# A layer norm in a transformer block, worked on rows or on a feature-major copy of x

## The chip, the cores and the metric

The kernel runs on one core of a Trainium2 chip. TensorE (PE) multiplies matrices, VectorE (DVE), ScalarE (ACT) and GpSimd (POOL) work element by element, and SyncE (SP) issues the DMAs. Each engine takes its instructions in the order in which the program wrote them; semaphores tie the engines together. The metric is the device time of one execution in microseconds, and less is better.

## The reference

One transformer block in float32 for 2048 tokens with 448 features. The modulation (shift sa, scale ca, gate ga, and the same three for the second half) comes from a small vector c:

```python
sa, ca, ga, sb, cb, gb = (silu(c) @ w_mod) split in six
h = layernorm(x) * (1 + ca) + sa
x = x + ga * attention(h)         # 16 heads of 28, each token sees itself and 255 before it
h = layernorm(x) * (1 + cb) + sb
x = x + gb * (mish(h @ w1 + b1) @ w2)     # 448 -> 1792 -> 448
```

`layernorm` subtracts a token's mean over its features and divides by the root of its variance plus 1e-5. The change concerns the first `h` alone.

## The kernel before

Tokens are taken in four groups of 512, each of four tiles of 128. Float32 products are made of a high and a low part of each operand, and a 448-deep product of a tile then takes 11 matmuls (`passes`); so every `h` is kept as a high part `hh` and a low part `hl`, with features in partitions: four chunks of 128 features (the last 64 of them twice) by 512 tokens.

The first layer norm of a group goes like this. The rows of x (`xin`, 128 tokens x 448 features, four tiles) are loaded; DVE makes mean and variance of each tile (`ln_stats`), POOL the inverse root (L234, L235, a power); DVE normalises the rows in place (L241), POOL copies the last 64 features behind them (L224). Then PE transposes them, four 128x128 blocks into one PSUM bank `tr` for each chunk of features (`tr_chunk`, L250); ACT applies scale and shift and rounds to the high part (`hT_hi`, L257), DVE applies scale and shift to the bank (`hT_y`, L254) and subtracts the high part (`hT_lo`, L262). Group 0 does the same in its own code at the start, while weights arrive.

From `hh` and `hl` come the tiles of q, k and v of the group. Seven tiles `qk_0` to `qk_6` hold q and k with features in partitions; ACT and DVE split them into `st`, which is stored to DRAM (`scr`) and loaded again head by head (`q`, `k`). Four tiles `qk_v` hold v, and ACT and DVE evict them into `v` (DVE's part is L369). The tiles alternate between two PSUM banks of the tag `mm`, so a tile can begin only when the one two before it has been evicted.

A head then takes: scores `sA` for the row maxima (L679) and the maxima `mx` on DVE (L681); their transposes `mt`, cast to `mr` on DVE (L689, L690) and written into the operand q by a small DMA (`q<-mr`); scores again with the maximum and the mask inside (`sB`); the exponentials `P` and `Ph` on ACT, the low part `Pl` on POOL (L731); the product with v (`pv`). The 16 heads of a group are cut into 48 units of work, 192 in all. Between the units stand pieces of other work: the q, k and v tiles of the next group and the output projection of the group before (`fill_main`, handed out by a credit that grows by `RATE` with each unit), and small loads and element-wise work (`fill_side`). The order of instructions on every engine is the order of the program. All DMAs but one go through SP's queue (`dma`, L59); those of the fillers are put into the list `later` and issued at given places. After the heads, the MLP runs to the end (from 430 us on).

At the start the order is: the first q and k tiles of group 0, their stores, the loads of the first heads; then v0, v1, `qk_1`, v2, v3, `qk_5`, `qk_2`, with the scores `sA` of the first heads in between.

## Time and profile before

| | us |
|---|---|
| median of 3 runs | 710.71 (709.77 to 712.46) |
| profiled execution | 710.72 |
| its span in the trace | 708.9 |
| PE, DVE, ACT, POOL busy | 686.6, 385.2, 391.1, 327.0 |
| PE's 48 transposes of x in groups 1 to 3, busy | 7.3 |
| `hT_hi` on ACT, 16 in all, busy | 12.4 |
| `hT_y` (14) and `hT_lo` (16) on DVE, busy | 11.4 and 11.1 |
| normalisation of rows on DVE (12), busy | 11.2 |

The page shows one execution. A line of a group gives busy time, mean ns of one, and the engine's idle time before it with what ended it. The timeline gives start, duration and instruction, and in brackets how long the engine had been idle and what released it. Neighbouring instructions of one kind are drawn together (x4).

### The profile page before, as it was taken

How to read it: one execution, taken by the hardware profiler on the slowest of the kernel's cores; microseconds unless marked ns; L12 is line 12 of the kernel's file. 1: busy time of each engine (PE TensorE's matmuls, PEld its weight loads, DVE VectorE, ACT ScalarE, POOL GpSimd, SP SyncE). 2: the span in 40 equal slices, each digit the busy share in tenths (PEclk: the TensorE clock that was granted, in tenths of full speed). 3: DMA queues.
4: the chain of work that ended last, by engine and by line, in shares of the span. 5: the costliest groups of instructions: out<-in, count | busy, mean ns of one | idle time of the engine just before them, and what ended most of it. 6: DMA issues, size and time to landing. Idle time of an engine off the chain costs nothing.

```text
span 708.9 us, 12034 instructions
## 1 busy us (share of the span) xinstructions
PE 686.6 (97%) x4001; PEld 589.5 (83%) x4001; DVE 385.2 (54%) x1031; ACT 391.1 (55%) x740; POOL 327.0 (46%) x358
## 2 busy tenths in 40 slices
PE   9899999999999999999999799999999999999996
PEld 8677788888898788898887688888888888888885
DVE  5588667688664888555768744351324332532112
ACT  3628778767766858767877874343223322422221
POOL 6626779586766777666778947222010000000002
PEclk9999999999999999999999999999999999999999
DMA  7865764454662462763774155810250035001001
GB/s 211 253 226 181 226 198 150 137 161 150 192 216 66 153 207 76 195 200 92 226 216 128 54 192 166 228 29 1 104 119 1 0 104 119 1 12 41 1 1 52
DMA packets 75178, 90.16 MB, mean 127 GB/s; under 512 B 31535, under 2 KB 51741, under 8 KB 75117
## 3 DMA queue, kind: packets, MB, share of 16 engines
q1 hardware_dynamic: 74652, 89.39, 41.6%
q8 instruction: 32, 0.52, 0.3%
q14 instruction: 30, 0.24, 0.1%
q10 hardware_dynamic: 464, 0.00, 0.0%
HBM read 56.60 MB, written 32.51 MB: 126 GB/s over the span
## 4 chain that ended last, share of the span: by engine, by line
PE 71%; issue 11%; DVE 8%; ACT 2%; DMA 1%; POOL 1%; POOLq 0%; DVEq 0%; ACTq 0%
PE z L912 16%; PE pv L741 9%; PE qk L315 8%; PE sA L679 5%; PE acc L1097 5%; PE acc L1095 5%; PE acc L1096 5%; PE sB L709 5%; PE wo L315 4%; PE qk_v L315 4%; PE sB L720 3%; DVE junk L681 3%; PE et L755 2%; DVE tr L254 1%; ACT P L723 1%
## 5 line engine op out<-in xcount | busy, mean ns | idle before, releaser
L731 POOL TENSOR_TENSOR Pl<-P,Ph 128x512 fp32r<-128x512 f32 (+2 forms) x192 | 234.3, 1227 | 84.3 <-ACT Ph L724 46.1
L681 DVE CUSTOM_DVE_ANT_0 junk<-sA,mask 128x384 f32<-128x384 f32 (+2 forms) x256 | 135.3, 528 | 96.8 <-PE sA L679 88.1
L723 ACT ACTIVATE P<-sB 128x512 f32<-128x512 f32 (+2 forms) x192 | 109.7, 572 | 64.1 <-PE sB L720 59.0
L920 DVE TENSOR_TENSOR al<-t,ah 128x512 fp32r<-128x512 f32 x56 | 38.7, 692 | 178.8 <-ACT ah L919 178.8
L918 ACT ACTIVATE t<-z,b1c 128x512 f32<-128x512 f32 x56 | 38.4, 686 | 165.2 <-PE z L912 161.5
L724 ACT ACTIVATE Ph<-sB 128x512 fp32r<-128x512 f32 (+2 forms) x192 | 109.4, 570 | 0.0
L679 PE MATMUL sA<-k,q 84*128 84x384 f32 (+2 forms) x256 | 100.9, 396 | 2.8 <-DVE mx L681 1.5
L912 PE MATMUL z<-hlf,w 128*128 128x512 f32 x224 | 88.5, 395 | 0.0
L912 PE MATMUL z<-hhf,w 128*128 128x512 f32 x224 | 88.5, 395 | 0.0
L1095 PE MATMUL acc<-w2h,ah 128*128 128x448 f32 x224 | 82.0, 366 | 0.0
L1097 PE MATMUL acc<-w2h,al 128*128 128x448 f32 x224 | 81.9, 366 | 0.0
L1096 PE MATMUL acc<-w2l,ah 128*128 128x448 f32 x224 | 81.5, 364 | 0.0
L741 PE MATMUL pv<-Ph,v 128*60 128x256 f32 (+2 forms) x352 | 76.5, 291 | 3.6 <-DVE o L749 2.3
L741 PE MATMUL pv<-Pl,v 128*60 128x256 f32 (+2 forms) x352 | 73.6, 283 | 2.3 <-POOL Pl L731 2.3
L709 PE MATMUL sB<-q,k 86*128 86x256 f32 (+1 forms) x352 | 74.0, 284 | 0.2 <-DMA q<-mr 0.2
L912 PE MATMUL z<-hhf,w1l 128*128 128x512 f32 x168 | 66.2, 394 | 0.0
L709 PEld LDWEIGHTS sB<-q,k 86*128 86x128 f32 x352 | 61.5, 189 | 1.8 <-issue 0.8
L741 PEld LDWEIGHTS pv<-Ph,v 128*60 128x60 f32 x352 | 45.3, 133 | 18.2 <-ACT o L747 3.2
L720 PE MATMUL sB<-fdmask,identr 128*128 128x128 bf16 (+1 forms) x320 | 60.0, 253 | 0.0
L679 PEld LDWEIGHTS sA<-k,q 84*128 84x128 f32 x256 | 48.9, 192 | 9.1 <-DVE mx L681 6.0
L1106 POOL TENSOR_TENSOR yo<-yo,x 128x448 f32<-128x448 f32 x3 | 3.5, 1211 | 114.9 <-DVE yo L1104 114.9
L741 PEld LDWEIGHTS pv<-Pl,v 128*60 128x60 f32 x352 | 45.0, 131 | 10.8 <-POOL Pl L731 3.9
(161 smaller groups left out, 1291.6 us busy)
## 6 DMA issues: line engine op xcount, KB each, us to landing
scr<-st SPq DMA_DIRECT2D x24, 512.0 KB
k<-scr SPq DMA_DIRECT2D x48, 252.0 KB
q<-scr SPq DMA_DIRECT2D x64, 168.0 KB
scr<-st SPq DMA_DIRECT2D x32, 256.0 KB
x<-x1d SPq DMA_DIRECT2D x10, 448.0 KB
xin<-in_A_x_dram SPq DMA_DIRECT2D x8, 448.0 KB
xr<-in_A_x_dram SPq DMA_DIRECT2D x16, 224.0 KB
x1d<-xr SPq DMA_DIRECT2D x16, 224.0 KB
```

Of the source, the lines that this page charges most:

```text
L315: PE.matmul(p, b, a, start=(n == 0), stop=(n == 10))
L679: PE.matmul(p[:, c0:384], q[0:84, t * 128:(t + 1) * 128], k[0:84, t * 128 + c0:t * 128 + 384], start=True, stop=True)
L681: DVE.tensor_tensor_reduce(out=junk[:, c0:384], in0=p[:, c0:384], in1=mask[:, c0:384], scale=1.0, scalar=-3.0e38, op0=ALU.add, op1=ALU.max ...
L709: PE.matmul(p[:, c:c + 128 * (t1 - t0)], k[:, jj * 128:(jj + 1) * 128], q[:, t0 * 128:t1 * 128], start=(n == 0), stop=False, skip_group_ch ...
L723: ACT.activation(P[:, c0:], p[:, c0:], AF.Exp, scale=SCALE)
L724: ACT.activation(Ph[u][:, c0:], p[:, c0:], AF.Exp, scale=SCALE)
L731: eng.tensor_tensor(Pl[u][:, a:b], Pt[u][:, a:b], Ph[u][:, a:b].bitcast(F32), op=ALU.subtract)
L741: PE.matmul(pv[0:60, t0 * 128:t1 * 128], V[j % NV][:, h, :], P[u][:, c:c + 128 * (t1 - t0)], start=(P is Ph and b == 0 and n == 0), stop=F ...
L912: PE.matmul(zb[n], ps[m][1], ps[m][0], start=(m == 0), stop=(m == 10))
L1095: PE.matmul(p, ah[n][:, ts], w2h[f], start=(f == 0), stop=False)
L1096: PE.matmul(p, ah[n][:, ts], w2l[f], start=False, stop=False)
L1097: PE.matmul(p, al[n][:, ts], w2h[f], start=False, stop=(f == NF - 1))
```

## The change

The host passes a second copy `xt` of x, with features in partitions: for each group four chunks of 128 features (the last 64 twice) by 512 tokens. For groups 1 to 3 the rows are still loaded, but only for their statistics (`gen_rows`): four tiles `xr` of 128x448 in two buffers. Means and inverse roots (`mva`, 128x8) are stored to a small DRAM array `xms` and loaded back as two tiles `mb` in which every partition holds the value of all 512 tokens. Then (`gen_ln1`) POOL subtracts the mean from each chunk of `xt`, DVE multiplies by 1 + ca and by the inverse root, ACT adds sa and rounds to the high part `hx`, and DVE makes the low part `hy`. `hx` and `hy` have buffers of their own, one each, and the next group's are written when the last tiles that read them are in (`free`). The fillers wait for `ready`. Gone are the transposes, the rows' normalisation, POOL's copies, and the early load of group 1's `xin`; `RATE` of groups 1 and 2 is 0.83 and was 0.91. The statistics of group 1 are driven from the nine steps `fill0` at the start, those of group 2 and 3 from the units of the group two before. Line numbers shift: v's eviction on DVE is L369 before and L403 now, `Pl` L731 and L761.

```diff
-    x_load(0)
+    xin0 = qk.tile([128, 4, 512], F32, name="xin0", tag="hy")
+    for t in (0, 2):
+        dma(xin0[:, t:t + 2, 0:D], xf[t * 128:t * 128 + 256, :].rearrange("(t p) d -> p t d", p=128))
...
+    def gen_rows(g):
+        mv = qk.tile([128, 2, 4], F32, name=f"mva{g}", tag="mv", bufs=2)
+        rows = []
+
+        def load(t):
+            r = qk.tile([128, D], F32, name=f"xr{g}_{t}", tag="row", bufs=2)
+            later.append(lambda: dma(r, xf[g * GT + t * 128:g * GT + t * 128 + 128, :]))
+            rows.append(r)
+
+        load(0)
+        yield
+        load(1)
+        yield
+        for t in range(4):
+            flush()
+            ln_stats(rows[t], mv[:, :, t], qk, f"a{g}{t}")
+            if t < 2:
+                load(t + 2)
+            yield
+        POOL.tensor_scalar(mv[:, 1], mv[:, 1], EPS, None, op0=ALU.add)
+        POOL.tensor_tensor(mv[:, 1], mv[:, 1], mhalf, op=ALU.pow)
+        yield
+        later.append(lambda: dma(xms[g - 1].rearrange("a t p -> p (a t)"), mv))
+        yield
...
     def gen_ln1(g):
-        def xn_tiles():
-            return [xin[g][:, t] for t in range(4)]
-        for r in gen_ln([xin[g][:, t, 0:D] for t in range(4)], qk, xn_tiles, f"a{g}"):
-            if r:
-                XS[g] = r
+        drain(rows[g])
+        flush()
+        mb = [stg(qk, f"mb{g}_{a}") for a in range(2)]
+        ys = [stg(qk, f"xt{g}_{k}") for k in range(4)]
+        later.append(lambda: dma(ys[0], xt[g, 0]))
+        later.append(lambda: dma(mb[0], xms[g - 1, 0].rearrange("t p -> (t p)").partition_broadcast(128)))
+        yield
+        later.append(lambda: dma(ys[1], xt[g, 1]))
+        later.append(lambda: dma(mb[1], xms[g - 1, 1].rearrange("t p -> (t p)").partition_broadcast(128)))
+        yield
+        for k in (2, 3):
+            later.append(lambda k=k: dma(ys[k], xt[g, k]))
+        yield
+        yield
+        flush()
+        for k in range(5):
             yield "dve"
+            if k < 4:
+                POOL.tensor_tensor(ys[k], ys[k], mb[0], op=ALU.subtract)
+            if k:
+                DVE.scalar_tensor_tensor(ys[k - 1], ys[k - 1], cols[:, 1, k - 1:k], mb[1],
+                                         op0=ALU.mult, op1=ALU.mult)
+        while g not in free:
+            yield
+        hh, hl = HT[g] = new_H(g)
+        for k in range(5):
+            yield "dve"
+            if k < 4:
+                ACT.activation(hh[:, k], ys[k], AF.Identity, bias=cols[:, 0, k:k + 1])
+            if k:
+                DVE.scalar_tensor_tensor(hl[:, k - 1], ys[k - 1], cols[:, 0, k - 1:k],
+                                         hh[:, k - 1].bitcast(F32), op0=ALU.add, op1=ALU.subtract)
+        ready.add(g)
...
-    def gen_hT(g):
-        drain(ln1[g])
-        hh, hl = HT[g] = new_T(g, mid)
-        for ci in range(4):
-            p = bank("mm", 2, f"tr{g}{ci}")
-            tr_chunk(XS[g], ci, p)
-            pipe.add(2, lambda p=p, ci=ci: hT_hi(p, ci, hh, 0), lambda p=p, ci=ci: hT_lo(p, ci, hh, hl, 0))
-            yield 1.2
...
-    x_load(1)
     split_cols(*QCOLS[1], (DVE, DVE, None, None))
...
         if g + 1 < NG:
-            yield from gen_hT(g + 1)
+            while g + 1 not in ready:
+                yield
             yield from gen_qkv(g + 1, (0, 3, 4, 1) + VT)
...
-    RATE = {0: 0.56, 1: 0.91, 2: 0.91, 3: 0.65}
+    RATE = {0: 0.56, 1: 0.83, 2: 0.83, 3: 0.65}
...
     for _ in range(9):
         fill0()
+        next(rows[1], None)
...
+            if k == 2 and g < 2:
+                next(rows[g + 2], None)
```

The first place is DVE at the start of the attention, where v0 and v1 of group 0 are evicted (the first two rows with L369 before, L403 in the change). Before:

```order
L200 TENSOR_TENSOR wq_106<-wqs_111,wq_106 64x512
L369 TENSOR_TENSOR v_165<-qk_v_484,v_165 128x16x28
L369 TENSOR_TENSOR v_166<-qk_v_497,v_166 128x16x28
L681 ISA junk,mx_525<-sA_0_526,mask 128x128
L681 ISA mx_525 128x1
L220 BN_STATS sta_536<-xin_378 128x6
```

In the change, at the same place:

```order
L189 TENSOR_TENSOR wq_107<-wqs_112,wq_107 64x512
L209 BN_STATS sta_499<-xr_0_488 128x6
L210 BN_AGGR mva_487<-sta_499 128x2
L209 BN_STATS sta_510<-xr_1_494 128x6
L210 BN_AGGR mva_487<-sta_510 128x2
L403 TENSOR_TENSOR v_166<-qk_v_482,v_166 128x16x28
L209 BN_STATS sta_520<-xr_2_502 128x6
L210 BN_AGGR mva_487<-sta_520 128x2
L209 BN_STATS sta_526<-xr_3_513 128x6
L210 BN_AGGR mva_487<-sta_526 128x2
L403 TENSOR_TENSOR v_167<-qk_v_504,v_167 128x16x28
L711 ISA junk,mx_547<-sA_0_548,mask 128x128
```

The statistics of group 1's four row tiles stood between the row maxima of the first head and now stand ahead of both evictions.

The second place is SP's queue there. `q_1` and `k_3` are the operands of heads 2 and 3, `scr<-st_1` the store of the tile `qk_1`, and `q_0<-mr` the maxima of the first pair of heads. In the change:

```order
L59 DMA k_3_149<-scr 84x512
L59 DMA xr_0_488<-in_A_x_dram 128x448
L59 DMA xr_1_494<-in_A_x_dram 128x448
L59 DMA xr_2_502<-in_A_x_dram 128x448
L59 DMA xr_3_513<-in_A_x_dram 128x448
L59 DMA xms<-mva_487 128x8x1
L59 DMA xt_0_559<-in_xt_dram 128x512
L59 DMA mb_0_557<-xms 128x512
L59 DMA xt_1_560<-in_xt_dram 128x512
L59 DMA mb_1_558<-xms 128x512
L59 DMA scr<-st_1_545 128x2x512
```

Before, `scr<-st_1` follows k of head 3 at once, and the rows of group 1 (`xin_378`) are asked for ahead of the first store. The ten rows between are new here.

The third place is DVE between the scores of the second head and the cast of the maxima, in the change (`mb_1` is the inverse root in all partitions):

```order
L316 SCALAR_TENSOR_TENSOR xt_0_559<-xt_0_559,cols,mb_1_558 128x512
L711 ISA junk,mx_547<-sA_3_620,mask 128x384
L711 ISA mx_547 128x1
L403 TENSOR_TENSOR v_169<-qk_v_587,v_169 128x16x28
L316 SCALAR_TENSOR_TENSOR xt_1_560<-xt_1_560,cols,mb_1_558 128x512
L719 CAST mr_632<-mt_630 8x128
```

Before, the normalisations of rows (L241) stand at these places; now the products with `mb_1`, two of them ahead of the cast.

More of the change, by code (lines that the diff above doesn't have):

```diff
@@ L270, in adaln_block, with stg, new_H @@
     XS, HT = {}, {}
-    def gen_ln1(g):
-        def xn_tiles():
-            return [xin[g][:, t] for t in range(4)]
-        for r in gen_ln([xin[g][:, t, 0:D] for t in range(4)], qk, xn_tiles, f"a{g}"):
-            if r:
-                XS[g] = r
-            yield "dve"
+    def stg(pl, name):
+        return pl.tile([128, 512], F32, name=name, tag="stg", bufs=6)
+    free, ready = set(), set()
+    def new_H(g):
+        return (qk.tile([128, 4, GT], F32R, name=f"hx{g}", tag="hx"),
+                qk.tile([128, 4, GT], F32R, name=f"hy{g}", tag="hy"))
@@ L396, in adaln_block @@
     rs0 = st0.tile([128, 2, 4], F32, name="rs0")
-    xs0 = XS[0] = [xin[0][:, t] for t in range(4)]
+    xs0 = XS[0] = [xin0[:, t] for t in range(4)]
     for t in range(4):
@@ L527, in xr_tile @@
     def xr_tile(name):
-        return mid.tile([128, 512], F32, name=name, tag="xr", bufs=3)
-    def stg(pl, name):
-        return pl.tile([128, 512], F32, name=name, tag="stg", bufs=4)
+        return mid.tile([128, D], F32, name=name, tag="xr", bufs=3)
     def wm_load(i, k, pl, ws):
@@ L976, in side_step @@
             told[g] = next(side[g], None)
-    RATE = {0: 0.56, 1: 0.91, 2: 0.91, 3: 0.65}
+    RATE = {0: 0.56, 1: 0.83, 2: 0.83, 3: 0.65}
     FRONT = {0: 0, 1: 2, 2: 2, 3: 2}
+    rows = {g: gen_rows(g) for g in range(1, NG)}
     ln1 = {g: gen_ln1(g) for g in range(1, NG)}
@@ L992, in need @@
             pipe.step()
+            if g not in ready:
+                next(side[max(g - 1, 0)], None)
             try:
@@ L1192 @@
     arrays, args = {}, []
+    rows = [*range(D), *range(384, D)]
+    xt = _np.asarray(inputs["A_x"])[0].T[rows].reshape(4, 128, NG, GT).transpose(2, 0, 1, 3)
+    inputs = {**inputs, "xt": xt}
     for name in _INS:
```

28 lines of the change are left out of this document (7 added, 21 removed).

## The prediction

> **What bounds the kernel now.** I read the page's busy table first, then the stretches of the layer norms, then the opening in order of time.
>
> ```profile
> span 708.9 us, 12034 instructions
> PE 686.6 (97%) x4001; PEld 589.5 (83%) x4001; DVE 385.2 (54%) x1031; ACT 391.1 (55%) x740; POOL 327.0 (46%) x358
> ```
>
> TensorE is busy for 97% of the span, so nothing makes up later for time in which it stands still, and work taken off it counts if nothing else ends last there. The next view cuts the span; its columns after the stretch are its length and the busy time of PE, PEld, DVE, ACT and POOL.
>
> ```profile
> 29.50:65.00 35.50, 31.29 (x181) 24.48 (x180) 27.14 (x87) 17.70 (x38) 14.98 (x21) 1.00 0.61 209
> 169.00:180.00 11.00, 10.11 (x77) 8.64 (x76) 10.38 (x29) 10.05 (x20) 7.87 (x7) 1.00 0.35 101
> 271.00:282.00 11.00, 10.11 (x76) 8.57 (x75) 10.37 (x26) 10.01 (x19) 8.08 (x7) 1.00 0.32 100
> 430.00:709.00 279.00, 273.09 (x1263) 236.76 (x1261) 88.78 (x144) 86.80 (x136) 30.91 (x38) 1.00 0.21 58
> ```
>
> The two 11 us stretches hold the transposes of groups 2 and 3: DVE and ACT are as full there as PE. Those of group 1 end the first stretch, where PE idles 4.2 us. The last 279 us are the MLP, which the change leaves alone. In the opening, everything hangs on small things in order of time:
>
> ```profile
> 30.51 1.16 DVE L369 TENSOR_TENSOR v<-qk_v,v 128x448 fp32r<-128x448 f32 x2
> 31.19 0.50 PE L315 MATMUL qk<-hh,wq 128*128 128x512 f32 x1 [1.10 <-DVE v L369]
> 34.90 0.30 PE L679 MATMUL sA<-k,q 84*128 84x128 f32 x1 [0.91 <-DMA k<-scr]
> 35.03 0.42 PE L315 MATMUL qk_v<-wq,hh 128*128 128x448 f32 x1
> 47.98 0.33 PE L709 MATMUL sB<-q,k 86*128 86x384 f32 x1
> ```
>
> PE starts the tile after v0 and v1 (31.19) the moment that DVE has evicted v0 and a PSUM bank is free. The tile v2 (35.03) needs v1's bank. 47.98 is the first score tile with its row maximum, from which the exponentials and all later units run.
>
> **The change part by part.** *Transposes, the gain.* The groups of the lines view give busy time and mean ns:
>
> ```profile
> L250 PE MATMUL tr<-ident,xin 128*128 128x128 f32 x48 | 7.3, 274 | 1.6 <-DVE hl L262 1.6
> L241 DVE TENSOR_SCALAR xin<-xin,mva,rsa 128x448 f32<-128x448 f32 x12 | 11.2, 929 | 0.5 <-POOL rsa L235 0.5
> ```
>
> 48 times 274 ns would be 13 us, but starts count on a pipelined engine, not durations:
>
> ```profile
> 53.63 0.60 PE L250 MATMUL tr<-ident,xin 128*128 128x128 f32 x4
> 53.98 0.42 PE L679 MATMUL sA<-k,q 84*128 84x384 f32 x1
> ```
>
> Four take 0.35 us to the next start and up to 0.44 on the chain of waits, so twelve groups of four give 4.2 to 5.3 us; I take 4.9. A third of that lies where PE idled anyway, so I take off 0.5. The 1.6 us that PE waited for DVE's `hl` goes too: two reads of a tile in PSUM (L254, L262) become reads of SBUF off PE's path. Gain 6.0 us, bounds 3 (the stretches stay bound by DVE and ACT, which get 24 new full-width operations on DVE for 36 old ones) and 8.
>
> *Row loads on DVE's queue, the main loss.* Before, group 1's rows (`xin`) were asked for at 20.83, and DVE's statistics stand behind both v evictions and the first row maximum. Now, by the order of instructions, the rows `xr` are issued on SP only after the loads of heads 2 and 3, and on DVE the statistics of xr_0 and xr_1 stand ahead of v0's eviction, those of xr_2 and xr_3 ahead of v1's.
>
> ```profile
> GB/s 211 253 226 181 226 198 150 137 161 150 192 216 66 153 207 76 195 200 92 226 216 128 54 192 166 228 29 1 104 119 1 0 104 119 1 12 41 1 1 52
> ...
> 20.83 1.03 SPq L59 DMA_DIRECT2D xin<-in_A_x_dram  x2
> 31.70 0.32 SPq L59 DMA_DIRECT2D k<-scr  x1
> 41.14 0.39 SPq L59 DMA_DIRECT2D k<-scr  x1
> 35.55 0.62 DVE L220 BATCH_NORM_STATS2 sta<-xin 128x6 f32<-128x448 f32 x1
> 36.21 0.18 DVE L221 BATCH_NORM_AGGREGATE mva<-sta 128x2 f32<-128x6 f32 x1
> ```
>
> The last of those head loads was issued at 41.14 to 41.53, having waited for stores to land. 896 KB of `xin` no longer runs ahead of the stores, worth 0 to 3.6 us at 253 GB/s (the second of the page's 40 slices); I take 1.5. So xr_0 is issued at 40.0 and xr_1 at 40.4. A load lands 3.2 us after its issue (31.70 to PE's start at 34.90), so 43.6 for a slightly larger one, and 44.2. With 0.62 + 0.18 for each, DVE reaches v0's eviction at 45.0 and ends it at 45.6 (0.58 each): PE starts at 45.6 what it started at 31.19, 14.4 us late. The `row` tag has two buffers, so xr_2 can be asked for only when xr_0 has been read (44.2), and xr_3 at 45.0; they land at 47.8 and 48.6, statistics end at 49.4, v1's eviction at 50.0. v2 starts at 50.0, not 35.03: 15.0 us late.
>
> *The bounce through DRAM, on top.* Now `mva` goes through POOL's power, to DRAM as 1024 single numbers of 4 bytes, and back as two broadcasts; no row here has that store. Nearest is the load of c, 448 numbers of 4 bytes, issued at 0.72 and used at 5.03, that is 4.3 us.
>
> ```profile
> 40.64 0.23 POOL L234 TENSOR_SCALAR rsa<-mva 128x4 f32<-128x4 f32 x1 [8.89 <-DVE mva L221]
> 40.96 1.04 POOL L235 TENSOR_TENSOR rsa<-rsa,mhalf 128x4 f32<-128x4 f32 x1
> 0.72 0.46 ACTq L83 DMA_DIRECT2D cT<-in_c_dram  x1
> 5.03 0.20 ACT L168 ACTIVATE sT<-cT 112x4 f32<-112x4 f32 x1 [2.54 <-DMA cT<-in_c_dram]
> 44.80 0.27 DVE L689 CAST mr<-mt 8x128 fp32r<-8x128 f32 x1
> 45.09 1.48 SPq L59 DMA_DIRECT2D q<-mr  x2
> L731 POOL TENSOR_TENSOR Pl<-P,Ph 128x512 fp32r<-128x512 f32 x155 | 201.1, 1302 | 76.3 <-ACT Ph L724 40.6 <-PE pv L741 10.4 <-PE sA L679 7.9
> L920 DVE TENSOR_TENSOR al<-t,ah 128x512 fp32r<-128x512 f32 x56 | 38.7, 692 | 178.8 <-ACT ah L919 178.8
> ```
>
> Power done at 50.7; the store between 3.2 (any load) and 9.8 (4.3 scaled by 1024/448), taken as 5.0 since part of 4.3 is fixed: 55.9 with its issue. SP waits there for it, and all behind it wait: xt_1, the stores of st_1, then `q<-mr`. The means land 3.4 us later at 59.3. POOL subtracts xt_0 in 1.3 (a subtraction of this size, L731): 60.6. DVE then has, ahead of the cast of the row maximum, the product of xt_0 (0.69 as L920), a maximum (0.6), v3's eviction (0.6) and the product of xt_1 (0.69, its subtraction ready at 61.9): the cast starts at 63.4. From cast to score tile took 47.98 - 44.80 = 3.2, so 66.6 against 47.98: **18.6 us late**, in place of the 15.0 and not beside it. The bounds are 14.8 (relief 3.6, store 3.2) and 24 (no relief, store 9.8). PE's order up to there has the same number of rows as before, so nothing is caught up. For groups 2 and 3 the rows are read tens of units ahead and the bounce is hidden behind PE's fillers; if that cover failed, each would cost a store and a broadcast, some 8 us.
>
> The Trainium skill ("TensorE: Matmul & The Clock Gate", Part 1) says that an idle window of about 3.4 us puts TensorE at half its clock, and that the return takes about as long. By that page such a stall would end with a slow stretch, for which I estimate, from its figures, 1.7 us of lost work. No run here has idle time of that length after the start, so it is not in the sum.
>
> *POOL, the second loss.* Twelve subtractions at 1.30 replace twelve copies of 0.3. In groups 1 and 2 they stand between the `Pl` of units in which POOL is already back to back:
>
> ```profile
> L224 POOL COPY xin<-xin 128x64 f32<-128x64 f32 x16 | 5.0, 315 | 5.5 <-DVE xin L241 3.4 <-ACT xin L407 0.9 <-PE qk L315 0.7
> ...
> 142.33 3.90 POOL L731 TENSOR_TENSOR Pl<-P,Ph 128x512 fp32r<-128x512 f32 x3
> 143.67 0.45 PE L741 MATMUL pv<-Pl,v 128*60 128x256 f32 x2 [0.40 <-POOL Pl L731]
> ```
>
> PE already waits 0.40 for POOL there. Four times 1.3 less 4 x 0.3 is 4 us a group; POOL's idle time nearby takes most. I take 2.5 for both, bounds 0 and 6. ACT's four `hx` per group (from SBUF, not PSUM) replace four `hh` of the same size: nothing, with 10.05 of 11 us in its stretch as the cover that then goes. The changed rate of fillers moves PE's work, and removes none: nothing.
>
> Sum against the profiled run's own 710.72 (span 708.9 and 1.8 around it; the runs' median is 710.71): 710.7 + 18.6 - 6.0 + 2.5 = 725.8, rounded to **725.5**.
>
> **Rivals.** *Short bounce.* The store takes no longer than a load and the relief is whole: 14.8 in place of 18.6, so 722. For it: 1024 numbers are little data. Against it: 4.3 us for 448 of them.
>
> *DVE and POOL hold each other up.* L241 takes 498 ns at its shortest and 1493 at its longest, always the same shape:
>
> ```profile
> L241 DVE TENSOR_SCALAR xin<-xin,mva,rsa x12: 498/852/1493, 42.0 to 256.6; 128x448 f32<-128x448 f32 x12
> ```
>
> If each of the 16 new DVE operations of groups 2 and 3, which read two SBUF tiles, puts 1.0 us on POOL or itself, and half of that lies on the path: +8, so 733.5. Against it: these stretches lose the L241 that show it. The Trainium skill ("SBUF — State Buffer", section on the two separate sides) calls the port pair of the two engines an exclusive lock, the loser waiting out the whole instruction, also for DVE operations with two SBUF inputs. L241's longest of 1493 agrees with a wait of about one operation.
>
> *The other side: the rows come in time.* If xr_0 to xr_3 landed by 29, statistics would be done before v0 and v1 need evicting and the mean's broadcast by 41: no stall, and 710.7 - 6.0 + 2.5 = 707 (704 to 709). It decides where the loads are issued: from about 25 us on, each later us is a us lost, since DVE's statistics stand ahead of the evictions. For it: the removed `xin` leaves that place free. Against it: SP's rows start in the order of the program (31.70, 41.14, 45.09), and there the loads stand behind k of head 3.
>
> **How the numbers follow.** Forecast 0.73 (its own range 721 to 730), short bounce 0.09, mutual blocking 0.13, rows in time 0.05. The range 715 to 736 goes from the smallest stall with the largest gain (710.7 + 14.8 - 8 = 717, and a little for overlap of refilling) to the largest stall with a gain of 3 and a POOL loss of 4 (735.7). A measurement here can tell 0.5%, that is 3.6 us, from no change. Faster: the last rival, 0.04. Within: its upper end and the lowest stalls, 0.03. Slower: 0.93.
>
> **What would show it.** In the profile after: PE idle for some 14 us from 31, released by DVE's v eviction, and DVE's idle time there released by the load of `xr`; `sB` first at 64 to 68; the groups' `tr` gone from 53 to 63, 169 to 176 and 271 to 278; POOL's subtractions of about 1.3 among the `Pl`; everything from about 70 us on late by a constant less the gains. It is wrong if PE runs through 31 to 45, if the first `sB` is at 50, or if the stretches between 120 and 280 lose more than 6 us.

## The result and the profile after

The changed kernel takes 757.11 us (median of 4 runs, 756.62 to 761.02) against 711.17 us for the kernel before beside it (709.77 to 712.46): 1.066 of its time, with an interval of 1.062 to 1.070. The forecast was 725.5, with 736 as the upper end of the range. So the direction was right and the loss three times what was forecast: 46 us and not 15. The profiled execution took 756.62 us, 45.9 more than the one of before.

The head of the page, to be set beside that of before:

```profile
span 754.8 us, 11984 instructions
...
PE 693.9 (92%) x3953; PEld 595.5 (79%) x3953; DVE 383.4 (51%) x1019; ACT 390.5 (52%) x740; POOL 343.0 (45%) x358
...
PEclk9966998998999998999999999999999999999999
```

TensorE has 48 matmuls fewer, the transposes, and yet 7.3 us more of busy time (693.9 for 686.6); its idle time went from 22.3 to 60.9 us. Idle time is 38.6 of the 45.9 us. The rest is busy time made longer: PEclk has two 6s over the opening (third and fourth slice, 38 to 75 us), where before the granted clock stood at 1.00 in the stretch from 29.5 to 65.

**The opening.** TensorE, then DVE, then SP's queue, in order of time:

```profile
46.87 0.80 PE L349 MATMUL qk<-hx,wq 128*128 128x512 f32 x1 [16.37 <-DVE v L403]
...
71.30 0.38 PE L717 MATMUL mt<-ident,mx 128*8 128x128 f32 x1 [11.90 <-DVE mx L711]
...
77.21 0.34 PE L739 MATMUL sB<-q,k 86*128 86x384 f32 x1
```

```profile
44.73 0.63 DVE L209 BATCH_NORM_STATS2 sta<-xr 128x6 f32<-128x448 f32 x1 [13.84 <-DMA xr<-in_A_x_dram]
...
46.22 0.59 DVE L403 TENSOR_TENSOR v<-qk_v,v 128x448 fp32r<-128x448 f32 x1
...
69.18 1.59 DVE L316 SCALAR_TENSOR_TENSOR xt<-xt,cols,mb 128x512 f32<-128x512 f32 x1 [11.21 <-DMA mb<-xms]
...
73.40 0.27 DVE L719 CAST mr<-mt 8x128 fp32r<-8x128 f32 x1
```

```profile
40.83 5.61 SPq L59 DMA_DIRECT2D xr<-in_A_x_dram  x4
...
51.10 0.38 SPq L59 DMA_DIRECT2D xms<-mva  x1
...
63.86 0.33 SPq L59 DMA_DIRECT2D mb<-xms  x1
```

There are two waits. TensorE idles 16.37 us up to 46.87 for v0's eviction on DVE, and DVE idles 13.84 us in front of its statistics for the rows `xr`, which SP issued at 40.83. Then the small store of means and inverse roots is issued at 51.10, and the load that reads it back at 63.86: 12.75 us apart. DVE idles 11.21 us in front of its first product for that load, the row maxima stand behind it on DVE, and TensorE idles 11.90 us for them. The first score tile with its maximum starts at 77.21, where it started at 47.98.

The chain of waits names the same two places:

```profile
40.83 3.87 DMA xr<-in_A_x_dram
...
51.10 12.75 DMA xms<-mva
```

**Where the 45 us come in.** I took the first score tile `sA` of each head in both traces; the table gives by how much it starts later than in the kernel before. z is the first tile of the MLP.

| start of | before, us | later after the change, us | gained since the row above |
|---|---|---|---|
| head 0 | 34.9 | 16.8 | 16.8 |
| head 3 | 48.3 | 29.2 | 12.4 |
| head 12 | 88.7 | 30.5 | 1.3 |
| head 15 | 103.3 | 37.3 | 6.8 |
| head 21 | 136.9 | 36.4 | -0.9 |
| head 23 | 148.6 | 42.3 | 5.9 |
| head 37 | 238.7 | 40.7 | -1.6 |
| head 39 | 250.3 | 46.0 | 5.3 |
| z | 411.2 | 45.2 | -0.8 |

The lag comes in five steps. The first two are the opening. The others belong to groups 2 and 3, whose work was forecast to be covered. Between the steps the lag also drifts: after head 23 it goes on to 45.6 at head 31 and is back at 40.7 at head 37, with no long wait in between. The fillers of these groups are handed out more slowly than before (`RATE`), so a difference of a few us inside a group is not by itself a cost. Here is the third step in a view of stretches (columns: stretch, length, busy time of PE, PEld, DVE, ACT, POOL, granted clock, DMA share, GB/s), and under it TensorE and SP:

```profile
116.00:120.00 4.00, 4.00 (x28) 3.31 (x28) 2.97 (x12) 3.71 (x10) 2.71 (x4) 1.00 0.38 17
120.00:124.00 4.00, 4.00 (x27) 3.21 (x26) 1.66 (x7) 2.45 (x7) 2.55 (x3) 1.00 0.65 26
124.00:129.00 5.00, 0.88 (x5) 0.36 (x3) 0.24 (x2) 0.64 (x2) 1.26 (x1) 0.78 0.79 232
129.00:133.00 4.00, 3.80 (x14) 3.20 (x15) 0.58 (x3) 2.15 (x6) 1.01 (x1) 0.50 0.90 323
```

```profile
129.20 0.66 PE L739 MATMUL sB<-q,k 86*128 86x384 f32 x1 [4.32 <-DMA q<-mr]
...
182.83 0.66 PE L709 MATMUL sA<-k,q 84*128 84x384 f32 x1 [3.78 <-DMA k<-scr]
...
288.11 0.66 PE L709 MATMUL sA<-k,q 84*128 84x384 f32 x1 [2.91 <-DMA k<-scr]
```

```profile
112.86 0.39 SPq L59 DMA_DIRECT2D xms<-mva  x1
...
120.09 5.33 SPq L59 DMA_DIRECT2D q<-mr  x2
```

Group 2's store is issued at 112.86. From 116 to 124 the DMA engines are counted as busy for 0.38 and 0.65 of the time and move 17 to 26 GB/s; then they move 232 and 323. The `q<-mr` issued at 120.09 lands too late, and TensorE idles 4.32 us. After that it works at half clock: 14 matmuls in 4 us, where there were 28 before the wait. Heads 22 and 38 wait in the same way for `k<-scr`, 3.78 and 2.91 us.

The single packets of this trace tell more. The 1024 pieces of 4 bytes are noted with some 9 ns each, and nearly all of them start between 114 and 116 us. What is slow comes after them: a 2 KB packet of another transfer takes 92 ns on average from 112.9 to 116, 790 ns from 116 to 124, and 102 ns from 124 to 129. So the pieces do not fill the engines by their own time; for 8 us after them everything else crawls. Where they are held in these 8 us the trace does not show.

Group 3's store (issued at 217.09) has the same form, and the engines again move only 7 GB/s from 224 to 228. But little else is asked for there, and TensorE waits 0.44 us:

```profile
229.78 0.47 PE L739 MATMUL sB<-q,k 86*128 86x384 f32 x2 [0.44 <-DMA q<-mr]
```

That gave four suspects to take apart: the place of the row loads, the store of 4-byte pieces, the queue in which k's small store and load stand, and the clock.

### The profile page after: what moved, and what is told of

It reads as the page before. It is cut to its first block, busy times and chain, and to the rows that moved or that the text cites. A ratio compares the mean times of both kernels' runs of the same rounds, so it can differ in the third digit from the quotient of the medians.

```text
span 754.8 us, 11984 instructions
## 1 busy us (share of the span) xinstructions
PE 693.9 (92%) x3953; PEld 595.5 (79%) x3953; DVE 383.4 (51%) x1019; ACT 390.5 (52%) x740; POOL 343.0 (45%) x358
## 4 chain that ended last, share of the span: by engine, by line
PE 66%; issue 11%; DMA 11%; DVE 6%; POOL 2%; ACT 2%; SPq 1%; POOLq 0%; ACTq 0%; DVEq 0%
PE z L942 15%; PE pv L771 8%; PE qk L349 5%; PE sA L709 4%; PE acc L1135 4%; PE acc L1133 4%; PE acc L1134 4%; PE sB L739 4%; PE wo L349 4%; PE qk_v L349 4%; DMA xms<-mva 3%; PE sB L750 3%; DMA scr<-st 2%; DMA q<-mr 2%; DVE junk L711 2%
## 5 line engine op out<-in xcount | busy, mean ns | idle before, releaser
L761 POOL TENSOR_TENSOR Pl<-P,Ph 128x512 fp32r<-128x512 f32 (+2 forms) x192 | 236.8, 1240 | 95.5 <-ACT Ph L754 63.8
L771 PE MATMUL pv<-Ph,v 128*60 128x256 f32 (+2 forms) x352 | 78.4, 297 | 3.7 <-DVE o L779 2.3
L739 PE MATMUL sB<-q,k 86*128 86x256 f32 (+1 forms) x352 | 76.0, 290 | 6.2 <-DMA q<-mr 6.2
L709 PEld LDWEIGHTS sA<-k,q 84*128 84x128 f32 x256 | 50.5, 199 | 16.0 <-issue 7.1
L349 PE MATMUL qk<-hx,wq 128*128 128x512 f32 x100 | 41.7, 417 | 16.4 <-DVE v L403 16.4
```

The lines of the kernel that those rows point to most:

```text
L349: PE.matmul(p, b, a, start=(n == 0), stop=(n == 10))
L709: PE.matmul(p[:, c0:384], q[0:84, t * 128:(t + 1) * 128], k[0:84, t * 128 + c0:t * 128 + 384], start=True, stop=True)
L739: PE.matmul(p[:, c:c + 128 * (t1 - t0)], k[:, jj * 128:(jj + 1) * 128], q[:, t0 * 128:t1 * 128], start=(n == 0), stop=False, skip_group_ch ...
L761: eng.tensor_tensor(Pl[u][:, a:b], Pt[u][:, a:b], Ph[u][:, a:b].bitcast(F32), op=ALU.subtract)
L771: PE.matmul(pv[0:60, t0 * 128:t1 * 128], V[j % NV][:, h, :], P[u][:, c:c + 128 * (t1 - t0)], start=(P is Ph and b == 0 and n == 0), stop=F ...
```

## The experiments

### The store by itself, and each opening wait by itself

First the store was put alone into the kernel before: a tile of zeros, 128 partitions by 8, written to DRAM at unit 24, with nothing that reads it. Once it goes out in the layout of the change, 1024 pieces of 4 bytes; once as 128 pieces of 32 bytes.

```diff
+    pbd = dram.tile([2, 4, 128], F32, name="pbd")     # second probe: [128, 8]
+    pb = qk.tile([128, 8], F32, name="pb", tag="pb")
+    POOL.memset(pb, 0.0)
...
+        if u == 24:
+            dma(pbd.rearrange("a t p -> p (a t)"), pb)  # second probe: dma(pbd, pb)
```

> The kernel before, with one store added that nobody reads: 1024 numbers of 4 bytes from a 128x8 tile to DRAM, each to an address of its own, at the place where the changed kernel stores the means of group 2 (behind k of head 10's loads, ahead of the stores of qk_3). Theory A (the small pieces hold the DMA engines for some 10 us, whatever waits for the store): almost no other packets for about 9 us after it, the next maxima q<-mr land late, PE waits about 4 us there as in the changed kernel, and the time rises by 4 to 7 us, to about 716. Theory B (PE's loss there comes from the other loads and stores that the change added or moved): no gap, within 1 us of before.

> The same added store at the same place, the same 4 KB, but each partition's 8 numbers go to one piece of 32 bytes: 128 pieces, not 1024. Theory A with a cost for each piece: an eighth of the hold, about 1.3 us, and PE hidden from it: 711 to 712. If a store to DRAM of any form stops the queue there, as much as with 1024 pieces, 715 to 718.

The 4-byte store costs 720.52 us, 1.012 of before (1.006 to 1.018); the 32-byte store 712.26, 1.001 (0.999 to 1.002), which can't be told from no change. The same 4 KB in the same place cost some 8.5 us or nothing. SP's queue and TensorE with the 4-byte store; then SP's queue with the 32-byte store; then the kernel before:

```profile
83.52 0.82 SPq L59 DMA_DIRECT2D pbd<-pb  x1
...
93.13 3.17 SPq L59 DMA_DIRECT2D q<-mr  x2
```

```profile
98.17 0.64 PE L713 MATMUL sB<-q,k 86*128 86x384 f32 x1 [4.46 <-DMA q<-mr]
```

```profile
82.91 0.67 SPq L59 DMA_DIRECT2D pbd<-pb  x1
...
88.49 1.48 SPq L59 DMA_DIRECT2D q<-mr  x2
```

```profile
89.58 1.49 SPq L59 DMA_DIRECT2D q<-mr  x2
```

Nobody reads `pbd`, and yet TensorE idles 4.46 us for the next `q<-mr`. The stretch from 88 to 95 us with the 4-byte store and in the kernel before, columns as above:

```profile
88.00:95.00 7.00, 5.72 (x36) 4.04 (x34) 2.83 (x11) 4.42 (x10) 4.21 (x4) 1.00 0.94 112
```

```profile
88.00:95.00 7.00, 7.00 (x46) 5.22 (x44) 3.29 (x15) 5.28 (x13) 4.05 (x5) 1.00 0.69 206
```

The DMA engines are counted as busier than before (0.94 for 0.69) and move about half (112 GB/s for 206): the small pieces delay whatever shares the engines with them. The loss is above the 4 to 7 us that theory A expected. The step in the start of the heads is 7.1 us by head 15 and 8.1 at head 63. It is the third step of the table above (6.8), made in a kernel that has nothing else of the change.

Then each of the two opening waits was mended in the changed kernel. The first run loads group 1's four row tiles in the place in which the kernel before loaded `xin`, all at once, into buffers that are free there. The second has TensorE transpose the 128x8 means and roots, so that the store goes out as eight pieces of 512 bytes, in all three groups.

```diff
-            r = qk.tile([128, D], F32, name=f"xr{g}_{t}", tag="row", bufs=2)
+            r = stg(qk, f"xr{g}_{t}")[:, 0:D]           # group 1 only
...
+    rows = {g: gen_rows(g) for g in range(1, NG)}       # ahead of the first st stores
+    next(rows[1])
+    flush()
```

```diff
-        later.append(lambda: dma(xms[g - 1].rearrange("a t p -> p (a t)"), mv))
+        if g > 1:
+            yield
+        p = bank("tr", 1, f"mw{g}")
+        PE.transpose(p[0:8, 0:128], mv.rearrange("p a t -> p (a t)"), ident)
+        mw = qk.tile([8, 128], F32, name=f"mw{g}", tag="mw")
+        ACT.activation(mw, p[0:8, 0:128], AF.Copy)
+        yield
+        later.append(lambda: dma(xms[g - 1].rearrange("a t p -> (a t) p"), mw))
```

> The changed kernel, with one thing undone: the four row tiles of group 1 are asked for ahead of the first stores of q and k, where the kernel before asked for them (into four buffers that the means and xt use later). The order on DVE stays, statistics ahead of v0's eviction. Forecast's theory (DVE's queue is held by the late row loads): PE's wait of 16.4 us at 30.5 falls below 2; the store of the means goes out behind the loads of head 3 at about 41, and the first sB starts at about 66 to 68 instead of 77.2, so 746 (743 to 749). Rival (the wait at 30 is for something else in v's eviction, such as its ACT half): 755 to 758.

> The changed kernel with one thing changed: the means and inverse roots (128x8) are turned on PE and stored as 8 pieces of 512 bytes instead of 1024 of 4 bytes, in all three groups. The row loads stay late. Theory A: the first wait of PE stays at 16 us; from the store to the first load of the means 3 us instead of 12.7; first sB at about 68 instead of 77.2; the step of 5 to 7 us between heads 12 and 15 is gone; time about 741 (738 to 745). Theory B (a round trip through DRAM and the broadcasts cost this much in any form): 752 to 758.

With the rows early, 745.00 us, 1.046 (1.039 to 1.053); with the store in eight pieces, 737.79, 1.036 (1.028 to 1.044). Beside the 757.11 of the change they win 12 and 19 us, as the first theory of each run has it; the time with the large pieces is just below its range. TensorE with the rows early, then SP's queue and TensorE with the large pieces (line numbers have moved by a few in both):

```profile
33.60 0.50 PE L356 MATMUL qk<-hx,wq 128*128 128x512 f32 x1 [4.02 <-DVE v L410]
...
58.27 0.38 PE L727 MATMUL mt<-ident,mx 128*8 128x128 f32 x1 [12.77 <-DVE mx L721]
```

```profile
50.80 0.29 SPq L59 DMA_DIRECT2D xms<-mw  x1
...
52.02 0.33 SPq L59 DMA_DIRECT2D mb<-xms  x1
```

```profile
45.98 0.79 PE L356 MATMUL qk<-hx,wq 128*128 128x512 f32 x1 [16.10 <-DVE v L410]
...
60.12 0.27 PE L724 MATMUL mt<-ident,mx 128*8 128x128 f32 x1 [1.43 <-DVE mx L718]
```

Each mends its own wait and leaves the other: 16.37 us become 4.02 (below 2 was expected) with the second wait at 12.77; and 11.90 become 1.43 with the first at 16.10. From the store to the load that reads it are 1.2 us instead of 12.75. In starts of heads, the early rows bring head 0 to 2.6 us late in place of 16.8. The large pieces bring head 3 to 17.3 in place of 29.2, and their step from head 12 to head 15 is 0.4 us, not 6.8. The steps at heads 21 to 23 and 37 to 39 stay in both (store in large pieces: 7.1 and 4.5), so they have another cause.

### Both mendings, the queue, and the clock

> Both mendings in the changed kernel: group 1's rows asked for early, and the means stored in pieces of 512 bytes. If the row loads and the small store are two separate causes, their gains add: PE's first wait below 4 us, the second (12 us) gone too, first sB at 51 to 54, time 757 - 12 - 19 = about 724 (721 to 728). If one hides behind the other: 733 or more. The steps of 4 to 7 us at heads 22 and 38 stay.

Both together: 731.50 us, 1.028 (1.023 to 1.033). The waits that are left in the opening:

```profile
35.44 0.38 PE L302 MATMUL mw<-ident,mva 128*8 128x128 f32 x1 [5.03 <-POOL mva L297]
...
51.82 0.37 PE L734 MATMUL mt<-ident,mx 128*8 128x128 f32 x1 [3.31 <-DVE mx L728]
```

The first is of the experiment's own making: the transpose of the means stands in TensorE's order ahead of work that was ready, and waits there for POOL's power. Head 3 is 9.3 us late. If the gains of 12.1 and 19.3 simply added, the time would be 725.7; the result lies between the two expectations. A mending has a place in a queue too.

For the steps at heads 22 and 38, one edit on top of it: the store of a finished q and k tile goes to the front of the list of waiting DMAs, ahead of the loads of `xt`, of means and of rows.

```diff
-            later.append(put)
+            later.insert(0, put)
```

> The same, and in addition a finished q or k tile's store to DRAM goes to the head of the list of waiting DMAs, not to its end, so that it is issued ahead of xt, the means and the row loads that wait there. Theory C (heads 22 and 38 wait for k because its store stands in SP's queue behind some 1.2 MB of xt, means and rows, and k's load right behind the store): the steps of 7.1 and 4.5 us there shrink to below 2 each, time about 715 (712 to 719). Rival (the added bytes hold the DMA engines wherever the store stands, or PE waits there for POOL, whose subtractions of the mean stand between the Pl): 721 to 728.

It gives 728.72 us, 1.024 (1.020 to 1.028), far from the 715 of theory C. The step at heads 21 to 23 goes from 5.9 to 5.3, that at 37 to 39 from 5.2 to 1.7; in the opening the same edit costs, for head 3 is now 12.9 us late in place of 9.3. SP's load of k for head 22 and TensorE's wait for it:

```profile
152.25 0.35 SPq L59 DMA_DIRECT2D k<-scr  x1
...
159.59 0.66 PE L726 MATMUL sA<-k,q 84*128 84x384 f32 x1 [2.39 <-DMA k<-scr]
```

The order of issue accounts for most of the step at 38 and little of that at 22. The intervals of the two kernels overlap, so the 2.8 us between their medians are not shown by the times; the move of the step is in the traces. Why k still comes late at 22 can be read from SP's queue in this trace: the store goes out at 147.74, but k's load is issued at 152.25, behind five loads of `xt`, means and rows (148.69 to 151.31, 1.2 MB), and TensorE starts on k only at 159.59. So the store no longer stands behind these loads, and k's load still does. No run moved that load.

For the clock, transposes of the identity matrix into a spare bank were put into the two opening waits of the changed kernel, 140 and 105 of them. They compute nothing that is used, and keep TensorE working.

```diff
+    wb2 = bank("pv", 1, "warm2")
...
+            for _ in range(140):                        # ahead of qk_1
+                PE.transpose(wb2[:, 0:128], ident, ident)
...
+            for _ in range(105):                        # ahead of the first mt
+                PE.transpose(wb2[:, 0:128], ident, ident)
```

> The changed kernel, with 140 transposes of the identity (never read) put ahead of the tile qk_1, where PE stands still for 16.4 us, and 105 ahead of the first turning of the maxima, where it stands 11.9 us; at 0.11 us each they end about when the waits end. If the low granted clock after the waits (0.53 in 47 to 52 us, 0.75 in 71 to 80) comes from the idle time, the 11 matmuls behind the first wait start 0.23 us apart instead of 0.43, those behind the second as well, the clock reads 1.0 there, and 2 to 4 us are won: 753 to 755. If the clock has no part in the loss: 757.

756.87 us, 1.064 (1.059 to 1.068): the same as the change. The stretch behind the first wait, in the change and then with the transposes, and under them the stretch behind the second wait with the transposes:

```profile
47.00:52.00 5.00, 5.00 (x13) 3.96 (x14) 2.08 (x5) 0.10 (x1) 1.27 (x2) 0.53 0.23 75
```

```profile
47.00:52.00 5.00, 4.72 (x24) 3.92 (x23) 3.38 (x11) 0.60 (x1) 1.27 (x2) 1.00 0.20 50
...
71.00:75.00 4.00, 4.00 (x13) 3.24 (x13) 3.50 (x8) 0.60 (x1) 2.98 (x2) 0.57 0.07 19
```

Behind the first wait the granted clock is 0.53 in the change and 1.00 with the transposes; matmuls of that tile start 0.43 us apart and 0.23 apart, and 24 fit in the stretch that held 13. So the half clock is real; but TensorE only reaches the next wait sooner, whose end is set by the means. Behind the second wait the run did not do what was expected: the transposes ended early, TensorE still idled 1.96 us, and the clock fell to 0.57 (0.50 in the change). The MLP starts 44.2 us late in place of 45.2. So the half clock behind the first wait costs nothing in the times; what it costs behind the second, where no other wait follows at once, was not measured.

### Can the stall be ordered away?

Three kernels move the pieces of the last mending. In `mended`, group 1's statistics are driven between the row maxima of group 0's first heads, with the transpose of the means one step later, so that neither v's evictions on DVE nor TensorE stand behind them. In `mended2` the statistics come right behind v1's eviction, and the loads of the rows of groups 2 and 3 begin four heads later. `mended3` also holds back `xt` and the means of group 1 until the first `q<-mr` are issued.

```diff
+            if next(rows[1], 0) == 0:                   # mended: in the loop of the first scores
+                side_step(0)
...
+    for _ in range(5):                                  # mended2: behind the nine steps fill0
+        next(rows[1])
...
-            if k == 2 and g < 2:                        # mended2
+            if k == 2 and g < 2 and s % H >= 4:
...
-            if next(rows[1], 0) == 0:                   # mended3
+            if next(rows[1], 0) == 0 and i == 2:
```

> All three mendings (rows early, pieces of 512 bytes, stores first), and in addition the statistics of group 1 stand between the row maxima, behind v0's and v1's evictions, as in the kernel before. If late rows, small store and late k stores were all that cost, the start is as before (first sB at 48 to 49), and what is left is the forecast's gain from the transposes less POOL's share: 6.0 - 2.5, so 706 to 711, against 712 for the kernel before on this chip. If 24 new operations on DVE and 12 on POOL cost as much as the transposes: 711 to 714. If something else still stands in the way: above 715.

> The last kernel (723) with two things placed otherwise. Its own trace shows POOL's low parts waiting 3.0 us at head 4 behind a subtraction of the mean whose load was late, and q<-mr late at head 16 behind loads. Here the four statistics of group 1 stand right behind v1's eviction, where DVE was idle for 3.7 us before, so the means go out some 5 us earlier; and the row loads of groups 2 and 3 begin four heads later, away from xt and the means of the group ahead. If order alone is left as the cause: the step of 5.2 us at heads 4 and 5 and the 7.2 us at heads 16 to 18 are gone, the waits at heads 21 and 37 below 1 us, time 708 to 713 against 711 to 712 before. If the added operations and 3.6 MB of loads cost it wherever they stand: 716 to 722.

> The last kernel (724, whose PE stands 7.0 us at 53.3 for the first q<-mr) with one thing moved: the loads of xt and the means of group 1 (1.5 MB) are issued behind the first q<-mr, a store of the means and the loads of head 4, not ahead of them. Theory D (a small load that PE needs at once lands late when a megabyte has been issued before it): the 7.0 us wait and the half clock behind it (2 us) go, first sB at 48 to 49, and the lag at heads 3 and 4 falls from 7.7 to below 2; time 714 to 718. Rival (q<-mr is late because DVE's cast of the maxima is, or POOL's subtractions then hold the Pl for as long): 721 to 726.

All three take the same time: 723.41 us (1.018, 1.014 to 1.023), 723.97 (1.019, 1.015 to 1.022) and 723.41 (1.016, 1.013 to 1.020). For none of them does the time fall in the range in which order, or one late load, was all that was left; `mended2` is above its rival's range too. The place where it is lost moves. Lag of the heads, as above:

| start of head | 0 | 3 | 6 | 12 | 15 | 19 | 23 | 39 |
|---|---|---|---|---|---|---|---|---|
| mended | -0.4 | -0.8 | 5.0 | 3.7 | 4.0 | 11.3 | 13.6 | 12.9 |
| mended2 | -0.4 | 5.7 | 6.8 | 5.8 | 7.2 | 7.4 | 8.3 | 9.3 |
| mended3 | -1.1 | -1.8 | 4.7 | 2.9 | 3.7 | 10.0 | 12.1 | 13.2 |

Head 0 is in time in all of them, so the opening wait for v is gone. One row of TensorE for the next loss, in `mended`, `mended2` and `mended3` in this order, the last with the row of POOL behind it:

```profile
56.38 0.45 PE L787 MATMUL pv<-Pl,v 128*60 128x128 f32 x2 [2.98 <-POOL Pl L777]
```

```profile
53.34 0.66 PE L755 MATMUL sB<-q,k 86*128 86x384 f32 x1 [6.97 <-DMA q<-mr]
```

```profile
55.23 0.54 PE L787 MATMUL pv<-Pl,v 128*60 128x128 f32 x2 [2.62 <-POOL Pl L777]
```

```profile
52.69 1.26 POOL L327 TENSOR_TENSOR xt<-xt,mb 128x512 f32<-128x512 f32 x1 [3.20 <-DMA mb<-xms]
```

In `mended2` the 4 KB of `q<-mr` stand behind 1.5 MB of `xt` and means and TensorE idles 6.97 us. Where they are held back, as in `mended3`, heads up to 3 run ahead of the kernel before. Then POOL's first subtraction, which stands ahead of `Pl` in POOL's order, waits 3.20 us for the means, and TensorE idles 2.62 us for `Pl`, with half clock behind it. Each place that was tried for group 1's norm had a wait of its own.

The last pair leaves group 1 with rows and transposes, as before, and gives the new way (with stores of eight pieces) to groups 2 and 3 alone; the second of the two also has k's stores first and the row loads four heads later.

```diff
-    ln1 = {g: gen_ln1(g) for g in range(1, NG)}
+    rows = {g: gen_rows(g) for g in range(2, NG)}
+    ln1 = {g: gen_ln1(g) if g > 1 else gen_ln1_rows(g) for g in range(1, NG)}
```

> The same without the two orders: a finished q or k tile's store goes to the end of the waiting list, and the rows of the next but one group are asked for from the group's first head on. Theory C (k's store behind xt, means and rows): the waits for k at heads 22 and 38 come back with about 4 and 3 us and the half clock behind them, 7 and 4.5 us in all as in the kernel with 512-byte pieces; 717 to 721. If neither order matters without group 1's disturbance: as the last kernel, within 2 us.

> The new layer norm for groups 2 and 3 alone. Group 1 has the rows, transposes and evictions of the kernel before, at their places. The means are stored in pieces of 512 bytes, finished q and k tiles are stored first, row loads begin four heads into a group. No time limit is near here: rows are loaded a whole group ahead. If only group 1's place in the opening was wrong, the lag is 0 up to head 20 and the two groups bring what 16 of the 24 operations and 8 of 12 transposes are worth, two thirds of 6.0 - 2.5 from the forecast: 709 to 710 against 712. If the extra loads (xt and means, 3 MB in the two groups) cost as much at heads 21 to 28 and 37 as in the kernels above (some 7 us in mended2, against 5 us won there): 711 to 714.

723.64 us (1.017, 1.015 to 1.018) and 717.63 (1.007, 1.005 to 1.009). Both are above the ranges that were expected. The opening costs nothing now: head 6 is 0.2 us early, and 0.3 late. The largest steps that are left stand at the same two waits for k; the row of TensorE at head 22 in the plain kernel and in the other:

```profile
149.29 0.69 PE L742 MATMUL sA<-k,q 84*128 84x384 f32 x1 [4.69 <-DMA k<-scr]
```

```profile
147.20 0.66 PE L742 MATMUL sA<-k,q 84*128 84x384 f32 x1 [1.87 <-DMA k<-scr]
```

The step from head 21 to 23 is 9.2 us in the plain kernel, 3.4 in the other; that from 37 to 39 is 5.4 and 3.7. The two edits were not tried apart. This is the best version that was found, and it is still slower than the kernel before.

## Why the prediction was right and wrong

The MLP starts 45.2 us late, where the forecast's terms make 15.1 (18.6 less 6.0, plus 2.5). Of the 30 us that are missing, 10.6 are in the opening and 18.0 in the steps of groups 2 and 3, which the sum put at nothing.

**Right: the row loads on DVE's queue.** The forecast had `xr` issued at 40.0 (40.83 in the trace), v0 evicted late so that TensorE starts its next tile at 45.6 (46.87), 14.4 us late (head 0: 16.8), and POOL's power done at 50.7 (store issued at 51.10). The run with early rows shows the cause: it alone takes head 0 to 2.6 us.

**Wrong in size: the store.** The first step that failed is "the store between 3.2 (any load) and 9.8 (4.3 scaled by 1024/448), taken as 5.0". It took 12.75, above its upper bound. Means came 3.9 us after their issue (3.4 forecast), cast to score tile took 3.8 (3.2). The two products on DVE ahead of the cast took 1.59 and 1.77 us where the forecast had 0.69 for each; the mean of all twelve is in the groups view:

```profile
L316 DVE SCALAR_TENSOR_TENSOR xt<-xt,cols,mb 128x512 f32<-128x512 f32 x12 | 14.9, 1244 | 11.2 <-DMA mb<-xms 11.2
```

POOL's subtractions were right, 1313 ns for 1.30. So the first `sB` came 29.2 us late in place of 18.6: of these 10.6 the store is 7.8 and the two products are 2.0. (The stall's upper bound is 24.9 by the forecast's own terms, 18.6 + 1.5 + 4.8, and not 24; 29.2 is above both.) The mistake was to price a store of 4-byte pieces by the nearest load of them, scaled by the count: the upper bound was itself only that row made larger. The Trainium skill ("DMA: Bandwidth & Descriptors", Rules for kernel authors) says that a last dimension that is not contiguous becomes one descriptor for each element, and to rearrange it. The pair of probes agrees: the same 4 KB in the same place cost 8.5 us in 1024 pieces, and nothing visible in 128.

**Wrong: the cover for groups 2 and 3.** The second step that failed cost the most: "For groups 2 and 3 the rows are read tens of units ahead and the bounce is hidden behind PE's fillers". The latency of the bounce was hidden; nobody waited for its result. But the store held up the other transfers, and the next unit's own `q<-mr`, which has no filler in front of it, came late: 6.8 us for group 2, and 7 to 8 for the same store alone in the kernel before. For group 3's store the cover held, with 0.44 us of idle time. And in the list of DMAs the new loads stood ahead of k's stores and loads, 5.9 and 5.3 us more at heads 22 and 38. For head 38 the run with k's stores first shows it; for head 22 it is read from SP's queue. The price that the prediction gave for a failed cover, "some 8 us" for each, was near by luck: it was meant for a wait for the means, and nobody waited for them. The cover was sought on TensorE and not on SP's queue and the DMA engines, which the change loads too. These three steps are 18.0 of the 45. The prediction's own sign of being wrong was there: the stretches between 120 and 280 lost about 9 us, not under 6 (the lag goes from 37.5 at head 19 to 46.4 at head 43).

**Left out of the sum: the clock.** Every one of these waits is followed by a stretch at half clock: granted 0.53 from 47 to 52, 0.50 from 71 to 75 and from 129 to 133, and 0.50 again from 183 to 187 and from 288 to 292. The Trainium skill ("TensorE: Matmul & The Clock Gate", Part 1) has an idle window of about 3.4 us put TensorE at half its clock; this trace agrees for four of the five waits (0.43 us between starts and 0.23 behind the first), and the fifth, of 2.91 us, was shorter. Behind the first wait the half clock cost nothing in the times, since the next wait ends elsewhere. Behind the waits of groups 2 and 3 it makes a step longer than its idle time: 6.8 for an idle of 4.32, 5.9 for 3.78, 5.3 for 2.91. The clock records have half clock for 4.4, 5.4 and 5.9 us after these waits; half of that, added to the idle time, gives an estimate of 6.5, 6.5 and 5.9, near the steps. It was not measured apart there.

**The gain was not measured.** Between the waits, from head 15 to 21, 23 to 37 and 39 to z, the changed kernel wins 0.9, 1.6 and 0.8 us back, 3.3 in all, where 6.0 for the transposes less 2.5 for POOL made 3.5. With the store in large pieces the three stretches give 1.0, 1.7 and 1.9. That this is near the forecast shows little. Group 1's transposes stood between heads 4 and 8 before, where the lag does not fall (29.2 at head 3, 30.5 at head 12); no transposes stood between heads 15 and 21; and the slower fillers move the heads inside a group. No run measured the transposes alone.

**The rivals.** The short bounce was wrong in sign: the store is longer than the forecast, not shorter. Mutual blocking of DVE and POOL lengthened operations (the new products take 729 to 1793 ns, the same shape), but none of the five steps is its own; its part is the 2.0 us of the two products in the opening. The Trainium skill ("SBUF — State Buffer", section on the two separate sides) has a DVE operation with two SBUF inputs wait for POOL. The trace agrees: the three products with no POOL operation beside them take 729, 729 and 742 ns; the first two of the opening start 0.2 and 0.1 us after a subtraction on POOL and end 0.55 us after it ends. No run took this away. The rows in time, the other side, forecast no wait in the opening: with the rows early the kernel is still at 1.046, since TensorE then waits 12.77 us for the row maxima that stand behind the means. With the rows early and the store mended, heads 0 to 3 are in time or early in `mended` and `mended3`, and the sum is still not under before.

## What to carry to other kernels

Where an instruction that waits for a load is put into an in-order queue, ask what stands behind it: here PSUM evictions stood behind statistics, and TensorE idled 16 us for rows that it did not need. Look at the pieces of a small transfer and not at its bytes, and ask what else is in flight while it runs: the cover of its latency does not cover what it does to others. Of a change that takes a few us from a full engine, first price the new waits, each with a slow stretch of clock behind it.

## What the runs showed of the hardware

A store of 4 KB to DRAM in 1024 pieces of 4 bytes took 12.75 us until the load that depends on it was issued, and slowed other transfers for some 8 us (17 to 26 GB/s at a DMA share of 0.38 to 0.65). In eight pieces of 512 bytes it was 1.2 us, and 128 pieces of 32 bytes did not show in the time at all. Whether it is the count of pieces or their size was not separated, since both changed together. It cost TensorE 4.32 and 4.46 us of idle time in two places, and 0.44 in a third, where little else was asked for.

A short idle time can be enough for the half clock. In `mended` TensorE idled 1.96 us, and the stretches around it and after it (same columns as above) are these:

```profile
118.92 0.66 PE L755 MATMUL sB<-q,k 86*128 86x384 f32 x1 [1.96 <-DMA q<-mr]
```

```profile
115.49:118.90 3.41, 1.46 (x9) 0.97 (x8) 0.63 (x4) 1.01 (x3) 2.27 (x3) 1.00 0.80 239
...
120.00:124.00 4.00, 4.00 (x16) 3.37 (x16) 2.38 (x8) 2.13 (x6) 1.76 (x2) 0.50 0.20 56
124.00:128.00 4.00, 4.00 (x24) 3.42 (x22) 2.27 (x9) 2.97 (x6) 3.40 (x5) 0.78 0.00 0
```

From 120 to 124 the granted clock is 0.50, with TensorE busy throughout, and only in the next stretch does it come back. The Trainium skill ("TensorE: Matmul & The Clock Gate", Part 1) asks for at least one idle window of about 3.4 us; this wait was shorter, and half speed came all the same. In the view of busy time such a stretch looks full; the count of matmuls (16 in 4 us, 24 in the next) tells it.

A longer wait of the kernel before, 2.29 us, left the clock at 1.00:

```profile
407.24 0.45 PE L741 MATMUL pv<-Ph,v 128*60 128x128 f32 x2 [2.29 <-DVE o L749]
```

```profile
402.74:406.15 3.41, 2.21 (x20) 1.85 (x18) 1.68 (x5) 3.26 (x7) 3.23 (x4) 1.00 0.49 157
406.15:409.57 3.42, 2.33 (x19) 1.96 (x19) 2.10 (x4) 1.82 (x5) 1.30 (x2) 1.00 0.00 0
```

In these traces the granted clock changes in steps of 3.41 us (in the change the half clock lasts 17.07, 13.65 and 6.83 us in its first three places). Cut by these steps (in the kernel before counted on from the start of its clock record at 6.77 us), the 1.96 us lie in one piece, of which TensorE is busy for 1.46 us; the 2.29 us are spread over two, busy for 2.21 and 2.33. So what seems to count is the idle share of such a piece and not the length of one wait. This is read from the traces; no run varied it, and in `rows_early` a piece that was busy for 1.60 us (27.98 to 31.39) was not followed by half clock at once.
